# A fused sigmoid attention and top-1 expert layer: when first weights are loaded, which queue loads keys and values, where the item list is built, and when gate sums are issued

## The chip, the cores and the metric

The kernel runs on one core of a Trainium2 chip. The metric is the device time of one execution in microseconds (us), as a median of several runs. The core has a matrix engine (TensorE, "PE" in the profile; its weight loads are "PEld"), a vector engine (VectorE, "DVE"), an activation engine (ScalarE, "ACT"), a general engine (GpSimd, "POOL") and a sync engine (SyncE, "SP") that here only issues DMAs. Every engine executes its own instructions strictly in the order in which the program gave them to it, and waits where an instruction's inputs or its output buffer are not ready. "SPq" and "POOLq" (or POOL with DMA_DIRECT2D) in the profile are DMA issues by SP and by GpSimd.

## What is computed

```python
scores = q @ k.T / sqrt(64) - log(448)          # 8 batches, 12 heads, 448 x 64
x = sigmoid(scores) @ v                         # -> 3584 tokens of 768
logits = x @ w_gate                             # 8 experts
e = argmax(logits);  g = softmax(logits)[e]
out = g * (relu(x @ w1[e]) @ w2[e])             # 768 -> 1024 -> 768
```

## The kernel before

**Attention** (`attention`, L605) works on 48 pairs of heads, two pairs at a time: 24 units `u` of 7 steps each (`ST` = 7), 168 steps `s`. A step computes one seventh of the keys for two pairs: 8 score matmuls (L561), two sigmoids on ACT (L546), 8 value matmuls (L577). Pair `g` needs its keys and queries loaded (L509, four DMAs of 56 KB for each of the two), transposed by DVE (`turn`, L530), and its values loaded (L522, two DMAs of 112 KB). `READY` (L598) issues these by place in the unit: at `i` = 0 and 3 it turns keys of the next unit and loads keys and queries of the unit after that; at `i` = 1 and 4 it turns queries and loads values of the next unit. Keys, queries and values have four buffers each. `K_POOL` (L591) is the pair below which keys and values are issued by GpSimd instead of SP; queries are always SP's. In the steps before `START` = 70 only attention is computed, two steps at a time (even `s`); from then on it is interleaved with the experts' products.

**Gate.** When a unit ends, ACT and DVE split its output (L585, L586: `sh`, `sl`), DVE transposes it into token rows (L462) that SP stores (L466), and `gate_a` (L261) adds its part of the logits: four matmuls (L266) into a PSUM tile and one DVE instruction (L271 or L273) into `g16`. `stages_late` calls it at `i` == 2 of the next unit for `s` >= 70, `stages_early` by another rule before. After three units a batch `b` is done, and the stages b, c, c2, l, c3, d, d2, g, e (`stage`, L637) choose its commonest expert, rank the tokens, scatter records of them to DRAM (L392, four indirect DMAs of GpSimd), and read the batch's whole slot of tokens back (`load_slot`, L429: SP reads two register values, then issues four DMAs of 336 KB into `raw`). The PSUM tiles of the scores and of the gate stages come from one ring of four.

**Slots.** Seven slots follow, each one batch's worth of tokens with one expert's weights (`moe`, L200). A slot has 288 products (matmuls of 128x128 by 448): 8 groups of 18 for the first layer (L216), then three times two groups of 24 for the second (L239). After a first-layer group ACT and DVE make `hh` and `hl` (L223, L224); after a second-layer group DVE scales and transposes it (L251, L252). Groups alternate between two PSUM tiles, so the engine work after a group may take as long as the next group's matmuls before PE waits. `split_tokens` (L441) makes the token parts of the next slot: a DVE transpose into `whole` (two buffers), a cast, a subtraction; the first slot's subtractions are GpSimd's (L452), at the steps of `SPLITS` (L594).

**Weights** (`Weights`, L138) go through five buffers `wst`: `load(n)` issues SP DMAs (L159, 384 KB; L128, 512 KB) until n pieces are loaded, `ahead(n)` splits pieces until n are split (ACT cast L135, GpSimd subtraction L136) and keeps five loads in front of the piece being split. A load into a buffer waits until the subtraction that reads it is done. The first call, `ahead(0)`, comes with stage l of batch 1 (step 52), right behind that slot's four token DMAs; `FIRST` (L593) then splits three pieces at steps 63, 66 and 69.

**Order.** The generator `mo` runs all 7 x 288 = 2016 products, and the program takes from it by hand: `more(n)` issues the next n products, `until(n)` issues products until n are left. Each step from 70 on takes 14 (`MIX`), in two halves of seven, which leaves 490 when attention ends. `gate_a` and the other stages of a step with `i` > 0 are issued between the two halves.

**Item list.** Tokens whose expert is not their slot's are handled at the end as items of 256 rows. DVE builds the list of items on 128x112 tables: two running scans (L788), comparisons, sums (L790 to L805); PE moves it to one row (L809), DVE writes it as integers `li` (L811) and clears the row buffers (L991, L992). All engines read the count from it, SP the item numbers; SP loads two items' records (L847), GpSimd gathers token rows with two indirect DMAs for each (L827), DVE sorts them (`sort_large`, copies L851), and `split_rows` transposes and splits them (L866 to L871). This is issued with 470 (scans), 450, 430, 422 and 412 products left; the first item's gathers with 400 and 388 left; its sort with 330 left, the second item's gathers with 318 and 306, the splits with 288, 270 and 252, the second sort with 234. Two items, computed by `large`, and a loop for any others end the kernel.

Of the kernel before, what the change touches and what calls it, by code (L numbers as in the profile page):

```python
# [24 lines left out]
def tile_sigmoid_attention_top1_moe(  # L25
# [112 lines left out]
    class Weights:  # L138


        LOADS, PARTS = KF + NU // 2, KF + NU
# [354 lines left out]
    def load_pair(g):  # L496
        if g >= NG:
            return
        b, hp = divmod(g, NP)
        for nm, src in (("k", k), ("q", q)):  # L500
            t = apool.tile([P, S // 32, 32], F32, tag=nm + "n", bufs=4, name=f"{nm}n_{g}")
            for h in range(2):
                for f in range(D // 32):
                    a = 2 * h + f
                    if nm == "q":
                        eng = nc.scalar if g == 0 or g == 1 and a < 2 else nc.sync
                    else:
                        eng = nc.gpsimd if 1 <= g < K_POOL else nc.sync
                    eng.dma_start(  # L509
                        t[32 * a : 32 * (a + 1)],  # L510
                        src[b, 2 * hp + h, :, 32 * f : 32 * (f + 1)].rearrange("(j r) s -> r j s", r=32),
                    )
            ops[g, nm + "n"] = t

    def load_values(g):
        if g >= NG or (g, "v") in ops:
            return
        b, hp = divmod(g, NP)
        t = apool.tile([P, KC, D], F32, tag="vn", bufs=4, name=f"vn_{g}")
        for h in range(2):  # L520
            eng = nc.gpsimd if 4 <= g < K_POOL else nc.sync
            eng.dma_start(t[quarter(g, h)], v[b, 2 * hp + h].rearrange("(p c) d -> p c d", c=KC))  # L522
        ops[g, "v"] = t

    def turn(g, nm):

        if g >= NG:
            return
        t = apool.tile([P, S], F32, tag=nm + "t", bufs=4, name=f"{nm}t_{g}")
        nc.vector.transpose(t, ops.pop((g, nm + "n")).rearrange("p j s -> p (j s)"))  # L530
        ops[g, nm] = t

    def warm_up(n):

        ps = ps_moe.tile([P, 512], F32, tag="moe", name="ps_warm")
        for _ in range(n):
            nc.tensor.matmul(ps[:, :P], ones, ones, start=True, stop=True)
# [3 lines left out]
    ST = KC  # L541
    N_ST = NG // 2 * ST
# [9 lines left out]
    def scores(s):  # L552
        u, c = divmod(s, ST)
        two = [2 * u + n for n in range(2)]
        pss = [score_tile(f"{g}_{c}") for g in two]
        for g, ps in zip(two, pss):
            if s == 0 and g == 1:
                warm_up(FILL)
            for h in range(2):
                ks = ops[g, "k"][OWN[h]].rearrange("d (p c) -> d c p", c=KC)[:, c]  # L560
                nc.tensor.matmul(ps[quarter(g, h), :S], ks, ops[g, "q"][OWN[h]], start=True, stop=True)  # L561
        for g, ps in zip(two, pss):
            squash(g, c, ps)
# [24 lines left out]
            for g, pv in pvs:  # L588
                tokens(g, pv)

    WARM, FILL, K_POOL = 60, 20, 18  # L591
    START = 70
    FIRST = {START - 7: 1, START - 4: 2, START - 1: 3}  # L593
    SPLITS = (START - 10, START - 9, START - 7, START - 6, START - 4, START - 3)  # L594
    PB = NP // 2 * ST
    MIX = (7, 7)
# [8 lines left out]
    def attention():  # L605

        order = ExitStack()
        order.enter_context(tc.manual_schedule())
        warm_up(WARM)
        load_pair(0)  # L610
        load_pair(1)
        for g in range(2):
            turn(g, "k")
            turn(g, "q")
            load_values(g)
        nc.gpsimd.dma_start(wg, w_gate.rearrange("(t p) e -> p t e", p=P))
        setup()
        for g in (2, 3):
            load_pair(g)
            load_values(g)  # L620
        done_av = done_sc = 0

        def weigh_to(n):
            nonlocal done_av
            while done_av < min(n, N_ST):
                weighted(done_av)
                done_av += 1

        def score_to(n):
            nonlocal done_sc  # L630
            while done_sc < min(n, N_ST):
                scores(done_sc)
                done_sc += 1

        gate = {}

        def stage(what, b):  # L637
            g = gate.setdefault(b, {})
            if what == "b":
                g["oh"], g["z"] = gate_b(b)  # L640
            elif what == "c":
                g["c"] = gate_c(b, g["oh"], g["z"])
            elif what == "c2":
                g["lm"] = gate_c2(b, g["oh"], *g["c"])
            elif what == "c3":
                gate_c3(b, *g["c"][:2])
            elif what == "l" and b > 0:
                load_slot(b - 1, g["c"][2])
                if b == 1:
                    wts.ahead(0)  # L650
            elif what == "d":
                g["si"] = gate_d(b, g["lm"])
            elif what == "d2":
                gate_d2(b, g["si"])
            elif what == "g" and b > 0:
                g["gs"] = gate_g(b - 1)
            elif what == "e" and b > 0:
                gate_e(b - 1, g["gs"])

        LATE = {3: "b", 7: "c", 8: ("l", "c2"), 9: "c3", 10: "d", 12: ("d2", "g"), 14: "e"}  # L660
        LAST = {3: "b", 5: "c", 6: ("l", "c2"), 7: "c3", 8: "d", 9: ("d2", "g"), 10: "e"}
        EARLY = {5: "b", 7: ("c", "c2"), 9: ("l", "c3"), 11: "d", 13: ("d2", "g"), 15: "e"}
        FIRST_LATE = {5: "b", 10: "c", 11: ("l", "c2"), 12: "c3", 14: "d", 16: ("d2", "g"), 17: "e"}
        PLACES = {}
        for b in range(B):
            for r, what in (EARLY, EARLY, FIRST_LATE, LATE, LATE, LATE, LATE, LAST)[b].items():
                at = (b + 1) * PB + r
                at += at < START and at % 2
                PLACES.setdefault(at, []).extend((w, b) for w in ((what,) if isinstance(what, str) else what))

        summed = {}

        def stages_early(s):
            for u in range(START // ST):
                if summed.get(u) == s - 2:
                    gate_a(u)
            for w in PLACES.get(s, ()):
                stage(*w)

        def stages_late(s):  # L680
            u, i = divmod(s, ST)
            if i == 2 and u - 1 not in summed and u <= N_ST // ST:
                gate_a(u - 1)
            for w in PLACES.get(s, ()):
                stage(*w)

        for s in range(N_ST + 11):
            u, i = divmod(s, ST)
            a = u * ST
            if s in FIRST:  # L690
                wts.ahead(FIRST[s])
            if s < START:
                if s % 2 == 0:
                    weigh_to(min(s - 1, (done_av // ST + 1) * ST))
                    if done_av and done_av % ST == 0:
                        summed.setdefault(done_av // ST - 1, s)
                    stages_early(s)
                    score_to(s + 2)
            elif i == 0:
                stages_late(s)  # L700
                score_to(a + 2)
                weigh_to(a)
                score_to(a + 4)
            yield s, MIX[0]
            if s >= START:
                if i > 0:
                    stages_late(s)
                if i == 3:
                    weigh_to(a + 2)
                    score_to(a + 6)  # L710
                    weigh_to(a + 4)
                    score_to(a + 7)
                    weigh_to(a + 5)
            if s == 8:
                nc.gpsimd.tensor_copy(wgs[:, :, 0:E], wg)
                nc.gpsimd.tensor_sub(wgs[:, :, E : 2 * E], wg, wgs[:, :, 0:E].bitcast(F32))
            if i in READY and s < N_ST:
                READY[i](u)
            if s in SPLITS:
                split_tokens(0, SPLITS.index(s))  # L720
            yield s, MIX[1]
        order.close()

    wts = Weights([(lambda b=b: regs.get(b)) for b in range(B + 1)])
# [8 lines left out]
    def more(n):  # L733
        nonlocal left
        for _ in range(min(n, left)):
            next(mo)
            left -= 1

    def until(n):
        more(left - n)  # L740
# [42 lines left out]
    nc.vector.tensor_scalar(cut(0), cut(0), float(TS), None, op0=ALU.add)  # L783
    nc.vector.tensor_tensor(ek(4), ek(0), n_rec, op=ALU.is_lt)
    nc.vector.tensor_sub(few, few, big)
    more(20)
    for msk, cum in zip((big, few), rank):
        nc.vector.tensor_tensor_scan(cum, cut(3), msk, 0.0, op0=ALU.mult, op1=ALU.add)  # L788
    ends = rest.tile([P, 1], F32, name="ends")
# [211 lines left out]
    for get in gets[0]:  # L1001
        more(12)
        get()
    until(330)
    by_raw = xpool.tile([P, S // 32, KD, 32], F32R, tag="raw", bufs=1, name="by_raw")
    by_raw = by_raw.rearrange("p j t s -> p (j t s)")
    first = [by_raw[:, n * TL : (n + 1) * TL] for n in range(2 * KD - 2)]
# [84 lines left out]
```

## Time and profile before

| | |
|---|---|
| time, median of 3 runs | 835.1 us (834.96 to 835.94) |
| the profiled execution | 836.3 us; from its first to its last instruction 834.5 us |
| mean granted PE clock | 0.987 |
| busy: PE, PEld, DVE, ACT, POOL | 96%, 73%, 48%, 47%, 42% |
| DMA | 124.07 MB, mean 149 GB/s |
| first product of the slots (L216) starts | 153.10 us |
| last product of the slots (L239) starts | 755.99 us |

PE is busy nearly throughout, so time is won or lost where PE stands still. The table by stretches, the list of waits of PE and the timeline of single engines show those places; an engine's own wait is shown in brackets behind its instruction, with what ended it. Rows of the timeline that hold several instructions of a kind ("x4") give the whole run's length.

### The profile page before, as it was taken

To read this page: it belongs to the slowest core of one execution; us is meant where nothing else is said; L and a number is where in the kernel's file an instruction comes from. 1 tells how busy PE (TensorE), PEld (TensorE's weight loads), DVE (VectorE), ACT (ScalarE), POOL (GpSimd) and SP (SyncE) were. 2 spreads that over 40 slices of the span, in tenths; PEclk is the share of its full clock that TensorE was granted. 3 is DMA by queue.
4 is the path that set the end of the run, shared out by engine and by line. 5 is a ranking of instruction groups with operands and counts; after the bars stand their busy time and mean duration, and the time that the engine had idled before them with its cause. 6 is when DMAs were issued, how large, how long until landed. Compare 5 with 4: busy or idle time off the path is not lost. (4 is left out here: it accounts for less than half of the span.)

```text
span 834.5 us, 15673 instructions
## 1 busy us (share of the span) xinstructions
PE 805.0 (96%) x5568; PEld 612.9 (73%) x5568; DVE 400.0 (48%) x861; ACT 388.2 (47%) x709; POOL 349.6 (42%) x328
## 2 busy tenths in 40 slices
PE   9999986999999999999999999999999799999996
PEld 6545442777867876777768768777788698999996
DVE  2454644362546327453354525574276765224533
ACT  5676653563545536444544445356333233334441
POOL 9756324234332632235223333334354445565250
PEclk9999998999999999999999999999999899999998
DMA  9685698577477756488473983855267446546670
GB/s 193 141 182 120 153 180 180 125 155 183 104 172 148 187 117 148 108 186 169 116 167 78 194 199 93 183 129 152 72 154 171 127 113 165 157 107 167 199 217 35
DMA packets 324595, 124.07 MB, mean 149 GB/s; under 512 B 222174, under 2 KB 322478, under 8 KB 324512
## 3 DMA queue, kind: packets, MB, share of 16 engines
q1 hardware_dynamic: 316448, 112.52, 59.2%
q0 software_dynamic: 5280, 10.15, 4.2%
q8 instruction: 45, 0.74, 0.4%
q10 hardware_dynamic: 2784, 0.34, 0.3%
q14 instruction: 38, 0.31, 0.1%
HBM read 100.89 MB, written 22.48 MB: 148 GB/s over the span
## 5 line engine op out<-in xcount | busy, mean ns | idle before, releaser
L546 ACT ACTIVATE at<-sc,bias_s 128x448 f32<-128x448 f32 x336 | 188.1, 641 | 152.3 <-PE sc L561 151.4
L136 POOL TENSOR_TENSOR w1l<-wst,w1h 128x768 fp32r<-128x768 f32 x72 | 132.2, 1844 | 209.4 <-ACT w1h L135 195.0
L136 POOL TENSOR_TENSOR w2l<-wst,w2h 128x512 fp32r<-128x512 f32 x84 | 106.7, 1290 | 174.2 <-ACT w2h L135 169.4
L577 PE MATMUL av<-at,vn 64*64 64x448 f32 x1344 | 164.5, 545 | 6.9 <-DMA vn<-in_v_dram 6.9
L561 PE MATMUL sc<-qt,kt 64*64 64x448 f32 x1344 | 167.5, 553 | 3.7 <-DVE g L273 2.9
L216 PE MATMUL ps<-xh,w1h 128*128 128x448 f32 x336 | 124.7, 371 | 6.8 <-DVE hl L224 6.3
L561 PEld LDWEIGHTS sc<-qt,kt 64*64 64x64 f32 x1344 | 82.1, 193 | 60.8 <-issue 32.7
L239 PE MATMUL ps<-hh,w2h 128*128 128x448 f32 x336 | 123.3, 367 | 1.0 <-DVE ob L252 1.0
L216 PE MATMUL ps<-xl,w1h 128*128 128x448 f32 x336 | 124.0, 369 | 0.0
L216 PE MATMUL ps<-xh,w1l 128*128 128x448 f32 x336 | 123.9, 369 | 0.0
L239 PE MATMUL ps<-hh,w2l 128*128 128x448 f32 x336 | 123.5, 367 | 0.3 <-POOL w2l L136 0.3
L239 PE MATMUL ps<-hl,w2h 128*128 128x448 f32 x336 | 123.1, 366 | 0.0
L577 PEld LDWEIGHTS av<-at,vn 64*64 64x64 f32 x1344 | 60.6, 134 | 68.5 <-issue 45.9
L135 ACT CAST w2h<-wst 128x512 fp32r<-128x512 f32 x108 | 65.2, 622 | 58.4 <-PE ps L239 45.0
L223 ACT ACTIVATE hh<-ps 128x448 fp32r<-128x448 f32 x56 | 30.6, 547 | 122.8 <-PE ps L216 122.8
L251 DVE TENSOR_TENSOR ps<-ps,gt 128x448 f32<-128x448 f32 x42 | 26.4, 629 | 122.7 <-PE ps L239 122.6
L224 DVE SCALAR_TENSOR_TENSOR hl<-ps,hh 128x448 fp32r<-128x448 f32 x56 | 34.7, 619 | 93.2 <-ACT hh L223 93.2
L216 PEld LDWEIGHTS ps<-xh,w1h 128*128 128x128 f32 x336 | 63.5, 189 | 15.8 <-DVE hl L224 7.1
L239 PEld LDWEIGHTS ps<-hh,w2h 128*128 128x128 f32 x336 | 65.2, 194 | 8.8 <-issue 4.1
L239 PEld LDWEIGHTS ps<-hh,w2l 128*128 128x128 f32 x336 | 65.2, 194 | 7.0 <-issue 3.0
L239 PEld LDWEIGHTS ps<-hl,w2h 128*128 128x128 f32 x336 | 65.2, 194 | 6.6 <-issue 3.3
L216 PEld LDWEIGHTS ps<-xl,w1h 128*128 128x128 f32 x336 | 63.5, 189 | 8.8 <-issue 3.5
(163 smaller groups left out, 1008.4 us busy)
## 6 DMA issues: line engine op xcount, KB each, us to landing
wst<-in_moe_w_dram SPq DMA_DIRECT2D x72, 384.0 KB, 3.5
wst<-in_moe_w_dram SPq DMA_DIRECT2D x54, 512.0 KB, 4.4
x_tok<-xt SPq DMA_DIRECT2D x64, 168.0 KB, 2.9
qn<-in_q_dram SPq DMA_DIRECT2D x186, 56.0 KB, 2.6
raw<-x_tok SPq DMA_DIRECT2D x28, 336.0 KB, 6.5
out_dram<-ob SPq DMA_DIRECT2D x84, 112.0 KB, 2.4
vn<-in_v_dram SPq DMA_DIRECT2D x68, 112.0 KB, 3.5
kn<-in_k_dram SPq DMA_DIRECT2D x124, 56.0 KB, 3.0
```

The lines of the kernel that those rows point to most:

```text
L135: nc.scalar.copy(hi, st)
L136: eng.tensor_tensor(lo, st, hi.bitcast(F32), op=ALU.subtract)
L216: nc.tensor.matmul(ps[:, :S], a[:, ws], b_, start=(t == 0 and n == 0), stop=(t == KD - 1 and n == 2))
L223: nc.scalar.activation(hh[:, :S], ps[:, :S], AF.Relu)
L224: nc.vector.scalar_tensor_tensor(hl[:, :S], ps[:, :S], 0.0, hh[:, :S].bitcast(F32), op0=ALU.max, op1=ALU.subtract)
L239: nc.tensor.matmul(ps[:, :S], a, b_, start=(j == 0 and n == 0), stop=(j == KF - 1 and n == 2))
L251: nc.vector.tensor_tensor(ps[:, :S], ps[:, :S], gate_rows[b], op=ALU.mult)
L546: nc.scalar.activation(at, ps[:, :S], AF.Sigmoid, bias=bias_s, scale=SCALE)
L561: nc.tensor.matmul(ps[quarter(g, h), :S], ks, ops[g, "q"][OWN[h]], start=True, stop=True)
L577: nc.tensor.matmul(psv[g][OWN[h], :S], ops[g, "v"][rows, c, :], at[rows], start=(c == 0), stop=(c == KC - 1))
```

## The change

Four things differ. First, the first weights: stage l of batch 1 no longer calls `ahead(0)`. Instead five single loads are issued at steps 55, 58, 61, 63 and 65 (`LOADS`), and the three first splits come at steps 65, 67 and 69. Second, GpSimd issues the keys and values of pairs up to 21 instead of 17 (`K_POOL` 22). Third, the scans of the item list are issued with 330 products left instead of 470, and all that follows keeps its distances (310, 290, 282, 272; gathers with 260 and 248 left) up to the first sort, in front of which `until(330)` becomes `more(14)`: the sort comes with 234 left, the second item's gathers with 222 and 210, the splits with 192, 174 and 156, the second sort with 138. Fourth, `stages_late` calls `gate_a` at `i` == 1, one step (14 products) sooner.

```diff
-    WARM, FILL, K_POOL = 60, 20, 18
+    WARM, FILL, K_POOL = 60, 20, 22
     START = 70
-    FIRST = {START - 7: 1, START - 4: 2, START - 1: 3}
+    LOADS = (START - 15, START - 12, START - 9, START - 7, START - 5)
+    FIRST = (START - 5, START - 3, START - 1)
...
                 load_slot(b - 1, g["c"][2])
-                if b == 1:
-                    wts.ahead(0)
...
         def stages_late(s):
             u, i = divmod(s, ST)
-            if i == 2 and u - 1 not in summed and u <= N_ST // ST:
+            if i == 1 and u - 1 not in summed and u <= N_ST // ST:
                 gate_a(u - 1)
...
+            if s in LOADS:
+                wts.load(LOADS.index(s) + 1)
             if s in FIRST:
-                wts.ahead(FIRST[s])
+                wts.ahead(FIRST.index(s) + 1)
...
     nc.vector.tensor_sub(few, few, big)
-    more(20)
+    until(330)
     for msk, cum in zip((big, few), rank):
         nc.vector.tensor_tensor_scan(cum, cut(3), msk, 0.0, op0=ALU.mult, op1=ALU.add)
...
         more(12)
         get()
-    until(330)
+    more(14)
```

## The prediction, made before the changed kernel ran

> **What bounds the kernel now.** The page's row of PE by slices first, then windows where it drops, then PE's waits.
>
> ```profile
> PE   9999986999999999999999999999999799999996
> ```
> ```profile
> 99.60:115.30 15.70, 15.70 (x140) 1.00 0.96 189
> 115.30:153.05 37.75, 27.52 (x214) 0.91 0.77 160
> ```
> ```profile
> PE av L577 <- DMA vn<-in_v_dram: 6.9, 1, 6.9
> PE ps L216 <- DVE hl L224: 6.3, 2, 5.9
> PE sc L561 <- DVE g L273: 2.9, 1, 2.9
> PE pl L278 <- DVE g L273: 2.0, 2, 1.6
> ```
>
> PE is nearly always busy, so only its pauses are to be had. Four matter: two in the second window (6.9 and 2.9), where PE is busy for 27.52 of 37.75 us and the granted clock falls to 0.91; one of 5.9 in the tail; one of 1.6 at a gate sum. (A window's row has length, PE's busy time and instructions, granted clock, DMA share, GB/s; a wait's row total, times, longest.) The change touches all four.
>
> The first two, followed back through SP's timeline and DVE's:
>
> ```profile
> 101.18 1.92 SPq L435 DMA_DIRECT2D raw<-x_tok  x4
> 103.29 9.76 SPq L159 DMA_DIRECT2D wst<-in_moe_w_dram  x5
> 113.35 3.76 SPq L509 DMA_DIRECT2D kn<-in_k_dram  x4
> ...
> 133.69 1.11 SPq L522 DMA_DIRECT2D vn<-in_v_dram  x2
> 135.07 0.41 SPq L159 DMA_DIRECT2D wst<-in_moe_w_dram  x1
> ```
> ```profile
> 119.79 0.65 DVE L530 STREAM_TRANSPOSE kt<-kn 128x448 f32<-128x448 f32 x1 [6.27 <-DMA kn<-in_k_dram]
> ```
>
> Five weight loads hold SP for 9.76 us, where one alone takes 0.41. Behind them pair 19's keys are issued at 113.35; DVE waits for them 6.27 us, the gate sum stands behind that transpose, and PE waits 2.9. From there SP issues nearly without a pause and does not catch up: pair 19's values go out at 133.69, and PE waits 6.9 for them. So it is the order and pace of SP's queue that ends last here.
>
> **The change, part by part.** *First weights and pairs 18 to 21.* What it can be worth comes from the two windows: the one just before the stall, and the one up to the slots' first product. In the first, 140 matmuls of attention and gate took 15.70 us, 0.112 each. The 214 of the second would take 24.0 us at that pace, not 37.75: **13.7 us**, and the first product would start at 139.4 instead of 153.1. That is more than the two waits (9.8), since the slow clock goes too.
>
> Does nothing else come late? GpSimd's costs by line (20 to 100 us), its timeline, and the page's landing time:
>
> ```profile
> L509 POOL DMA_DIRECT2D kn<-in_k_dram x46 | 29.4, 656 | 1.8 <-DMA kn<-in_k_dram 0.9 <-DVE sl L586 0.9
> L522 POOL DMA_DIRECT2D vn<-in_v_dram x28 | 15.1, 551 | 22.0 <-PE av L577 13.5 <-PE pc L315 7.0 <-DMA kn<-in_k_dram 1.1
> ```
> ```profile
> 95.63 2.08 POOL L522 DMA_DIRECT2D vn<-in_v_dram  x4 [7.03 <-PE pc L315]
> ...
> 111.12 0.97 POOL L392 DMA_INDIRECT recs<-rec,si  x1 [0.30 <-issue]
> 123.72 1.14 POOL L452 TENSOR_TENSOR xl<-whole,xh 128x448 fp32r<-128x448 f32 x1 [11.64 <-DVE xh L451]
> ...
> 126.85 1.82 POOL L136 TENSOR_TENSOR w1l<-wst,w1h 128x768 fp32r<-128x768 f32 x1 [0.52 <-ACT w1h L135]
> ```
> ```profile
> vn<-in_v_dram POOLq DMA_DIRECT2D x28, 112.0 KB, 4.0
> ```
>
> Added to GpSimd are 16 key DMAs (16 x 0.656 = 10.5 us) and 8 value DMAs (8 x 0.551 = 4.4). Pairs 18's and 19's keys fall in the time around 95.63 in which GpSimd only waits, and are there before 105. Pairs 20's and 21's come behind the four scatters (the last ends at 112.1), which themselves wait for the ranks. Then two groups of keys and pairs 18's and 19's values take 2 x 2.6 + 2 x 1.1 = 7.4: issued by 119.5, landed 4.0 later at 123.5. PE wants them at step 66; step 60 begins at 115.3, and three double steps of 32 matmuls (3.6 each) later it is 126.1. It fits by 2.6. Next come two more values (2.2), six token subtractions (6 x 1.14 = 6.8) and three weight subtractions (3 x 1.82 = 5.5): 134.0, before 139.4. Queued behind a value load that waits for its buffer are those subtractions; for them wait the first products, and SP, whose sixth weight load needs the first subtraction's buffer. Behind that wait on SP stand keys and queries of pair 23, not turned before step 73. I count none of these, and 13.7 stays. Its ends: 7.5, if the transfers keep the pace they had (a rival, below), and 13.7, since nothing else may be late. Without its cover a late value costs PE what it is late.
>
> *Gate sums a step sooner.* PE's and DVE's timeline:
>
> ```profile
> 423.21 0.36 PE L266 MATMUL psg<-sh,wgs 128*16 128x448 f32 x1
> 423.41 0.37 PE L266 MATMUL psg<-sl,wgs 128*16 128x448 f32 x1
> ...
> 428.04 0.56 DVE L273 TENSOR_TENSOR g<-g,psg 16x448 f32<-16x448 f32 x1
> ...
> 428.65 0.42 PE L278 MATMUL pl<-ident,g 16*128 16x16 f32 x4 [1.61 <-DVE g L273]
> ...
> 429.00 2.56 PE L577 MATMUL av<-at,vn 64*64 64x448 f32 x16
> ...
> 431.32 2.62 PE L561 MATMUL sc<-qt,kt 64*64 64x448 f32 x16
> ...
> 433.75 1.68 PE L577 MATMUL av<-at,vn 64*64 64x448 f32 x16
> ```
>
> The sum stood in DVE's queue until 428.04, though its matmuls began at 423.21. 14 products (0.20 us each, by the starts of the two L266 rows) sooner is 2.8 us: more than the 1.61 of the wait, so it goes, and with it the slow groups behind it (2.56 and 2.62 against 1.68): 1.61 + 0.88 + 0.94 = **3.4**. The rest of L278's waits (0.4) I count at nothing: what DVE does next is late there anyway. The new wait would be PE's for `sl`, which now has 21 products (4.3 us) of cover instead of 35; for its two casts and two subtractions that is enough, so nothing. Ends 0 and 3.4.
>
> *The scans later.* The scans' own row, GpSimd beside them, the end of the list's sums; then ACT, GpSimd, DVE and PE where the scans are put:
>
> ```profile
> L788 DVE TENSOR_TENSOR_SCAN w2s<-w2s x2: 360/5282/10203, 647.0 to 657.1; 128x112 f32<-128x112 f32 x2
> ```
> ```profile
> 650.74 6.18 POOL L136 TENSOR_TENSOR w2l<-wst,w2h 128x512 fp32r<-128x512 f32 x5
> ```
> ```profile
> 660.13 0.15 DVE L803 TENSOR_SCALAR lf<-lf 128x1 f32<-128x1 f32 x1
> ```
> ```profile
> 689.30 2.29 ACT L135 CAST w1h<-wst 128x768 fp32r<-128x768 f32 x3
> ...
> 690.21 1.84 POOL L136 TENSOR_TENSOR w1l<-wst,w1h 128x768 fp32r<-128x768 f32 x1 [0.73 <-ACT w1h L135]
> ...
> 690.63 0.65 DVE L252 STREAM_TRANSPOSE ob<-ps 128x448 f32<-128x448 f32 x1
> ...
> 695.73 0.36 PE L239 MATMUL ps<-hh,w2h 128*128 128x448 f32 x1
> ```
>
> The second scan took 0.36 us; the first 10.2, ending as GpSimd's unbroken row of subtractions did (650.74 + 6.18 = 656.92). So it was blocked, not slow. At the new place (330 left) DVE reaches the scans at 691.2, on the clock of before, behind that L252, while three weight subtractions, all cast by 691.6, fill GpSimd from 690.21 to 695.8. I take it that the scan waits for their end again. The list's sums end 2.8 us after the scans (657.5 to 660.3); 0.6 more for L251 and L252 in place of one `hl`, 0.6 for the scans: 699.8. PE needs them with 290 products left, where 695.73 stands: idle 4.1. Before it was 5.9; the slow matmuls after either I take as equal: **1.8** gained. Ends: 5.9 (a gap is found) and -3.5 (a block as long as before). The Trainium skill, SBUF — State Buffer, section Who interferes with whom, says that a VectorE instruction with two SBUF inputs and a GpSimd one that reads SBUF exclude each other, for one whole instruction. By that alone a scan would enter between two subtractions, and the idle would be about 1 us less; the first scan's 10.2 us over several of them disagree.
>
> Without the gathers (L827) among the last slot's token splits, DVE is less late there; I add **1.0** for short waits before the new place (ends 0 and 1.3).
>
> *The first sort.* It now follows the second gather by 14 products (2.8 us) instead of 58. Gathers and sort copies, then ACT and GpSimd in that slot:
>
> ```profile
> L851 DVE COPY w2s<-xg x4: 547/904/2212, 691.2 to 707.9; 128x768 f32<-128x768 f32 x4
> ...
> DMA to landing us min/median/max: 4.3/4.4/4.5
> ```
> ```profile
> 712.52 0.54 ACT L223 ACTIVATE hh<-ps 128x448 fp32r<-128x448 f32 x1 [2.38 <-PE ps L216]
> ```
> ```profile
> 713.86 1.84 POOL L136 TENSOR_TENSOR w1l<-wst,w1h 128x768 fp32r<-128x768 f32 x1 [1.80 <-ACT w1h L135]
> ```
>
> The second gather queues on GpSimd behind a weight subtraction that ends 3.2 us after its group's `hh` began (712.52 to 715.70). It lands 4.4 later, the copy takes 0.55, and behind it on DVE stands the next group's `hl` (0.6), for whose PSUM tile PE waits: with 0.3 of hand-overs 9.1 us after that `hh`. PE wants it two groups on, 36 x 0.20 less the 0.2 by which `hh` trails: 7.1. A new idle of 2.0, with 0.6 for a slower clock behind it: **-2.6**. Ends 0 and -5.9 (both copies at their longest, 2.2). Moved along at no cost: the clears of the row buffers, two record loads on SP, the second item's splits and sort, which keep at least 48 products to their inputs.
>
> **Sum**: 13.7 + 3.4 + 1.8 + 1.0 - 2.6 = 17.3. The profiled execution took 836.3 (834.5 of span, 1.8 around it), 1.2 above the median of 835.1: 819.0 in its own terms, **817.8** as a median.
>
> **Rivals.**
> - *Transfers set the pace at START* (0.15). For it: the DMA share of 0.96 in the first window; against it: 0.77 in the second, while PE stood still. Up to the first product some 7.6 MB must move (token read, six weight loads, the pairs' loads, two token stores, by their sizes). At the windows' mean of about 172 GB/s that takes 44 us from 101.2: 145.6, so 7.5 gained instead of 13.7: **824**. The Trainium skill, DMA: Bandwidth & Descriptors, section Issuing engines are not separate DMA queues, takes this side: several issuers only save issue time, usually small. SP's 9.76 us for five issues is not small.
> - *The tail is free* (0.15): the scans find GpSimd idle and the gather is in time; 4.1 + 2.6 more: **811**.
> - *The tail is worse* (0.12): scans blocked as long as before; 5.3 less: **823**.
> - *GpSimd's queue holds the first product: slower* (0.04). Each value load may wait for its buffer; the waits seen sum to 22.0, one of them 7.0. Four of 7.0 put 28 us before the subtractions: 134.0 becomes 162, the first product 9 later than before, and with the rest **841**. It decides from some 23 us of added waits.
> - *The loads are spread but SP stays full* (0.04), the token read alone holding it, and queries come late as keys did: 2.9 lost again, **821**.
>
> The forecast itself has 0.50, and 814 to 822 as its own range; with the rivals and the unknown ends it is **811 to 826**. 0.2% is about what a measurement of this kernel can tell from no change: faster 0.94, same 0.02, slower 0.04.
>
> **What would show it.** Right: no wait of PE for `vn` or `g` at 100 to 140, the first L216 near 139, L509 and L522 of GpSimd there; no wait of L278 at 410; a PE wait of some 4 us with 290 products left; one of 2 for `hl` four groups into the last slot. Wrong: a first product after 145, a new PE wait for `kt` or `w1l`, or tail waits above 8 us together.

## The result, and the profile after

The changed kernel takes 815.74 us (median of four runs, 814.98 to 818.63) against 835.52 of the kernel before on the same chip: a ratio of 0.9767 (0.9739 to 0.9795). The forecast was 817.8. The profiled execution took 814.98, with a span of 813.2. It is the fastest of the four, 0.8 under their median; that of before (836.3) lies 0.8 above this 835.52, and 1.2 above the 835.1 that the prediction went by. So the two traces differ by 1.5 more than the medians do.

First the page of the changed kernel: PE by slices, and the clock granted to it.

```profile
PE   9999999999999999999999999999999988999996
...
PEclk9999999999999999999999999999999999999999
```

The gaps of before (86 in slices 6 and 7, the 7 in slice 32) are gone, and a shallow new one stands in slices 33 and 34. Next the windows of PE at the start of the slots (length, busy and instructions, clock, DMA share, GB/s):

```profile
99.60:115.30 15.70, 15.70 (x140) 1.00 0.91 179
115.30:139.00 23.70, 23.24 (x213) 1.00 1.02 226
```

The same 213 or 214 matmuls that took 37.75 us take 23.70, at a granted clock of 1.00, and the transfers now run at 226 GB/s instead of 160. Then PE's waits (total, times, longest):

```profile
PE pli L810 <- issue: 3.0, 1, 3.0
PE ps L216 <- DVE hl L224: 2.5, 2, 2.2
PE ps_warm L537 <- POOL ones L75: 1.0, 1, 1.0
PE sc L561 <- DVE lg L292: 0.9, 2, 0.6
PE ps L216 <- DVE xt L462: 0.5, 1, 0.5
```

The waits for `vn` (6.9), for `g` (2.9 and 2.0) and the 5.9 for `hl` are gone. Two are new: 2.95 for the list's matmuls, and 2.2 for `hl` behind the first sort.

To see where the time went I compare the start of the same product (L216 and L239 in PE's timeline, counted from the first) in the two traces. The number is by how much it starts sooner in the changed kernel:

| product | sooner by, us | what lies since the row above |
|---|---|---|
| 1 | 14.1 | first weights, pairs 18 to 21 |
| 800 | 14.4 | |
| 900 | 17.8 | the gate sum at 428 |
| 1566 | 18.1 | |
| 1604 | 26.3 | the scans' old stall is gone |
| 1710 | 28.2 | short waits of the last layer are gone |
| 1800 | 24.0 | the list's new wait |
| 1878 | 20.1 | the sort's new wait |
| 2016 | 20.1 | |

Between them these rows also hold work that only moved: three groups of transposes (`px`, 0.36 us each, 1.1 together) ran between products 1710 and 1800 before, and run between 1800 and 1878 now. Set right for them, the list cost 28.2 - 24.0 + 1.1 = 5.3, the sort 24.0 - 20.1 - 1.1 = 2.8. The list's own four matmuls (L810, 0.6) moved too, from between products 1566 and 1604 to between 1710 and 1800: 0.6 of the 8.2 gained there, and 0.6 of the 5.3 lost, are theirs.

After the slots PE's work takes the same time in both. The spans differ by 1.2 more than these 20.1: from the last scatter's issue to the end it was 834.5 - 827.54 = 7.0 before, and is 813.2 - 807.46 = 5.7 now. That is not chance: it is 6.95 in all five traces with `K_POOL` 18, and 5.7 to 6.0 in all eight with 22, the one in which nothing else was changed among them (5.9). The scatter lands 3.3 us after its issue began in both; what is shorter is a `DRAIN` of GpSimd at the kernel's end, the longest of these three (shortest, median and longest in ns), before and after:

```profile
L1087 POOLq DRAIN  x3: 46/115/6356, 827.3 to 834.2; - x3
```
```profile
L1088 POOLq DRAIN  x3: 46/115/5096, 807.2 to 812.9; - x3
```

So a microsecond at the end comes with the keys and values on GpSimd, and the prediction had no term for it. Why, no run shows.

### The profile page after: what moved, and what is told of

It is laid out like the page before. It is cut to its first block, busy times and chain, and to the rows that moved or that the text cites. A ratio compares the mean times of both kernels' runs of the same rounds, so it can differ in the third digit from the quotient of the medians.

```text
span 813.2 us, 15675 instructions
## 1 busy us (share of the span) xinstructions
PE 798.7 (98%) x5568; PEld 612.5 (75%) x5568; DVE 395.5 (49%) x861; ACT 388.1 (48%) x709; POOL 364.7 (45%) x352
## 5 line engine op out<-in xcount | busy, mean ns | idle before, releaser
L561 PE MATMUL sc<-qt,kt 64*64 64x448 f32 x1344 | 163.7, 550 | 1.0 <-DVE lg L292 0.9
L577 PE MATMUL av<-at,vn 64*64 64x448 f32 x1344 | 158.7, 539 | 0.0
L216 PE MATMUL ps<-xh,w1h 128*128 128x448 f32 x336 | 124.6, 371 | 2.9 <-DVE hl L224 2.5
L216 PE MATMUL ps<-xl,w1h 128*128 128x448 f32 x336 | 124.2, 369 | 0.0
L216 PE MATMUL ps<-xh,w1l 128*128 128x448 f32 x336 | 124.1, 369 | 0.0
L239 PE MATMUL ps<-hh,w2h 128*128 128x448 f32 x336 | 123.2, 367 | 0.0
L239 PE MATMUL ps<-hl,w2h 128*128 128x448 f32 x336 | 123.2, 367 | 0.0
L239 PE MATMUL ps<-hh,w2l 128*128 128x448 f32 x336 | 123.1, 366 | 0.0
L216 PEld LDWEIGHTS ps<-xh,w1h 128*128 128x128 f32 x336 | 63.6, 189 | 12.4 <-DVE hl L224 3.2
L239 PEld LDWEIGHTS ps<-hl,w2h 128*128 128x128 f32 x336 | 65.2, 194 | 7.1 <-issue 3.5
L239 PEld LDWEIGHTS ps<-hh,w2h 128*128 128x128 f32 x336 | 65.2, 194 | 7.1 <-issue 3.5
L216 PEld LDWEIGHTS ps<-xh,w1l 128*128 128x128 f32 x336 | 63.6, 189 | 8.9 <-issue 2.6
L216 PEld LDWEIGHTS ps<-xl,w1h 128*128 128x128 f32 x336 | 63.5, 189 | 8.6 <-issue 3.5
```

Of the source, the lines that this page charges most:

```text
L216: nc.tensor.matmul(ps[:, :S], a[:, ws], b_, start=(t == 0 and n == 0), stop=(t == KD - 1 and n == 2))
L239: nc.tensor.matmul(ps[:, :S], a, b_, start=(j == 0 and n == 0), stop=(j == KF - 1 and n == 2))
L577: nc.tensor.matmul(psv[g][OWN[h], :S], ops[g, "v"][rows, c, :], at[rows], start=(c == 0), stop=(c == KC - 1))
```

## The experiments

Gains by product are meant as in the table above, against the trace of before. The kernel before was timed beside each group: 834.89 with the first four, 839.01 with the shift and the three after the rows, 835.78 with the rows and the last two. Chips differ by that much, so a time is read by its ratio.

### The loads alone

```diff
-    FIRST = {START - 7: 1, START - 4: 2, START - 1: 3}
+    LOADS = (START - 15, START - 12, START - 9, START - 7, START - 5)
+    FIRST = (START - 5, START - 3, START - 1)
...
-                if b == 1:
-                    wts.ahead(0)
...
+            if s in LOADS:
+                wts.load(LOADS.index(s) + 1)
             if s in FIRST:
-                wts.ahead(FIRST[s])
+                wts.ahead(FIRST.index(s) + 1)
```

> The kernel before with only the weight loads spread; pairs 18 to 21 stay on SP. Theory (SP's pace): the five loads held SP 9.76 us in a row and five single ones take 5 x 0.41 = 2.1, so SP gets 7.7 back, the rest of its queue is as full as before: first product near 145.4 instead of 153.1, about 828 us. Rival (the burst alone makes the stall): first product near 139, about 821 us. Rival (SP stays full, values late again): first product above 150, about 833 us.

828.8 us, ratio 0.992 (0.9903 to 0.9938); first product at 147.06, 6.0 sooner. Windows and waits of this kernel:

```profile
115.30:147.06 31.76, 25.78 (x213) 0.89 0.79 179
```
```profile
PE av L577 <- DMA vn<-in_v_dram: 5.5, 1, 5.5
```

The keys come in time, so the wait for `g` is gone, but SP's queue is as full as before behind it, and the values are late again. The theory held, 1.7 short of its 7.7.

### Pairs 18 to 21 alone

```diff
-    WARM, FILL, K_POOL = 60, 20, 18
+    WARM, FILL, K_POOL = 60, 20, 22
```

> The kernel before with only pairs 18 to 21's keys and values on GpSimd; the five weight loads stay one behind the other. Theory (SP's pace): SP loses 4 x (3.76 + 1.11) = 19.5 us of issues, so the wait for values (6.9) goes with the slow clock; queries of pair 19 now stand behind the five loads where keys stood, so some of the 2.9 stays: first product at 141 to 144, about 824 to 826 us. Rival (the burst decides): a wait of 2.9 or more for queries and the loads late behind it, first product above 148, about 831 us. Rival (no burst needed, issuers decide): first product near 139, about 821 us.

823.29 us, ratio 0.9856 (0.9839 to 0.9872); first product at 142.09, 11.0 sooner. SP's timeline, then DVE's, of this kernel:

```profile
102.76 9.31 SPq L159 DMA_DIRECT2D wst<-in_moe_w_dram  x5
112.17 7.32 SPq L509 DMA_DIRECT2D qn<-in_q_dram  x8
```
```profile
121.49 0.65 DVE L530 STREAM_TRANSPOSE qt<-qn 128x448 f32<-128x448 f32 x1 [4.98 <-DMA qn<-in_q_dram]
```

As expected the queries stand where the keys stood: DVE waits 4.98 for them and PE 1.7 behind it. The five loads still cost, but less. The median gained 11.6, a little more than the 9 to 11 expected; about 1 of its trace's gain lies at the end, as said above. The two parts overlap: 6.0 and 11.0 alone, 14.1 together.

### The gate sums alone

```diff
-            if i == 2 and u - 1 not in summed and u <= N_ST // ST:
+            if i == 1 and u - 1 not in summed and u <= N_ST // ST:
```

> The kernel before with only the gate sums a step sooner. Theory: the wait of 1.6 for g at 428 and the slow groups behind it go, 3.4 us: about 831.7 us, and product by product no difference elsewhere. Rival (the wait moves to the casts sl, or to the next thing DVE is late with): 0 to 1.6 us, 833.5 to 835.

Two readings that do not agree. In its trace the gain from product 800 to 900 is 3.44, as forecast, and no wait of PE over 0.3 is new in it. But the median is 833.68 against 834.89, a ratio of 0.9982 (0.9970 to 0.9995): 1.2 us, at most 2.5, which is in the rival's range. The next experiment gives part of the reason: it keeps the old gate sums, and has the same wait at the same place. First before, then the kernel with the scans alone, windows of PE. They are cut where the granted clock can change in that trace, which is every 3.41 us (the last section shows from what):

```profile
426.36:429.77 3.41, 1.80 (x16) 1.00 0.87 221
429.77:433.19 3.42, 3.42 (x24) 0.50 0.97 254
```
```profile
424.39:427.80 3.41, 2.37 (x12) 1.00 0.85 187
427.80:431.21 3.41, 2.84 (x32) 1.00 0.89 229
```

In both PE stands still for 1.61 us. Before, all of it lies in one stretch of 3.41 us, in which PE is busy for 1.80, and the next stretch runs at half the clock: half of 3.41 is lost, 1.7. In the other trace the wait lies across the end of a stretch, PE is busy for 2.37 and 2.84, and the clock stays at 1.00. In the other three traces that keep this wait (the two experiments above, the shift below) it lies whole in a stretch too, with PE busy for 0.53 of it, and one stretch at 0.50 follows. So 1.6 of the 3.4 is there each time, and the other 1.7 or 1.8 only where the wait falls so. That is not the whole reason: if it falls so in four executions of five, some 3.0 is to be expected (an estimate from these traces), more than the 2.5. The traces compared are also the fastest of this kernel's ten executions (832.12) and a slow one of before; the rest is open.

### The scans alone

```diff
     nc.vector.tensor_sub(few, few, big)
-    more(20)
+    until(330)
...
         get()
-    until(330)
+    more(14)
```

> The kernel before with only the scans 160 products later and the first sort 14 products behind the second gather. Theory (three signed terms: the old stall of 5.9 with its slow matmuls is worth 7.4, short waits 1.9, the new list wait with its slow matmuls costs 4.2, the new sort wait 2.6): 2.5 us gained, about 832.6 us. Rival (the tail's moves are worth what was forecast, 1.8 + 1.0 - 2.6): 0.2 us, about 835 us. Rival (the tail's gain comes only with the earlier start, which changes how GpSimd and DVE meet): no gain or a loss.

834.74 us, ratio 0.9997 (0.9984 to 1.001): no difference. That fits the rival with the forecast's own 0.2, and as well the one by which the gain comes only with the earlier start. By product 8.2 come from the old stall (1.8 to 10.0) and 1.9 from the short waits; then both new waits take 9.5 (11.9 to 2.4), against 8.1 in the changed kernel's trace. The waits themselves are the same to 0.2 (2.95 and 2.38, there 2.95 and 2.22); what differs is the clock behind the second, one stretch of 3.41 us at 0.50 here and none there. The later place takes away a stall and makes two that cost as much.

### What blocks a scan

The first scan of before took 10.2 us and ended with GpSimd's row of subtractions; in the changed kernel the two scans took 1.1 and 2.0 beside such a row. One difference was seen between the two traces: before, the scan began at 646.97, inside GpSimd's last scatter issue (646.14 to 647.12). The first test moves its start behind that issue:

```diff
     more(20)
+    nc.vector.memset(xgs, 0.0)
     for msk, cum in zip((big, few), rank):
...
     nc.vector.memset(xg, 0.0)
-    nc.vector.memset(xgs, 0.0)
```

> The kernel before with one 0.70 us clear (xgs) moved ahead of the first scan, so that the scan begins some 0.7 us later, inside GpSimd's first weight subtraction instead of inside the DMA issue before it. Theory (a VectorE instruction that begins while GpSimd issues a DMA gets no turn until the row of subtractions ends; one that begins inside a subtraction enters at the next boundary): both scans end by about 651 instead of 657, PE's wait for hl of 5 to 5.9 falls under 1, about 829 to 830 us. Rival (the length of the row decides): the scans end at the row's end as before, the wait grows by 0.5, no change or slower. Rival (chance from run to run): the wait falls in this look, the times spread as before.

838.35 against 839.01, ratio 1.000 (0.9981 to 1.0018); PE's wait is 5.06, so it neither fell under 1 nor grew. GpSimd's and DVE's timeline, and the scans by their shortest, mean and longest in ns:

```profile
648.82 3.66 POOL L136 TENSOR_TENSOR w1l<-wst,w1h 128x768 fp32r<-128x768 f32 x2
652.42 6.38 POOL L136 TENSOR_TENSOR w2l<-wst,w2h 128x512 fp32r<-128x512 f32 x5
```
```profile
649.48 8.25 DVE L789 TENSOR_TENSOR_SCAN w2s<-w2s 128x112 f32<-128x112 f32 x2
```
```profile
L789 DVE TENSOR_TENSOR_SCAN w2s<-w2s x2: 1379/4166/6952, 649.5 to 656.4; 128x112 f32<-128x112 f32 x2
```

The scan began inside the first subtraction and still waited 7.0, past four boundaries between subtractions. The theory that a start inside a DMA issue is needed falls. Nor did the shift change anything in a whole kernel: the kernels with the loads, the pairs and the gate sums alone keep the scans where they were. There the first scan begins inside the scatter's issue as before, and yet it gets its turn behind the fifth of the row's seven subtractions, the very place at which the shifted one does. In the kernel with the pairs alone:

```profile
L788 DVE TENSOR_TENSOR_SCAN w2s<-w2s x2: 1383/4549/7715, 635.8 to 643.4; 128x112 f32<-128x112 f32 x2
```

PE's wait is 5.0 to 5.1 in these three. So the 10.2 and the 5.9 that the prediction started from are what this one execution of before showed. The second test measures the row by itself, on tiles of its own ahead of the changed kernel's work. Four forms run three times each; "early" and "late" are as "ready", with six casts on ACT in front of the row or one in front of each subtraction:

```diff
...
+        def start():
+            nc.gpsimd.tensor_copy(go, cum[1])
+        def scans():
+            for c in cum:
+                nc.vector.tensor_tensor_scan(c, one, go, 0.0, op0=ALU.mult, op1=ALU.add)
+        def low(n, h):
+            nc.gpsimd.tensor_tensor(lows[n], src, highs[h].bitcast(F32), op=ALU.subtract)
+        def ready():
+            start()
+            scans()
+            for n in range(6):
+                low(n, n)
...
+        def issue():
+            start()
+            scans()
+            nc.gpsimd.dma_start(aside, one)
+            for n in range(6):
+                low(n, n)
```

> The changed kernel with four probes ahead of its first work, three times each: two scans (128x112) on VectorE that begin as a row of six GpSimd subtractions (128x512) begins. Forms: inputs ready long before (ready); the six casts that feed the row done before it (early); each cast ending while the subtraction before its own runs (late); a DMA issue between the scans' start and the row (issue). Theory A (a waiting VectorE instruction enters at a boundary only where GpSimd's next instruction was not yet ready when the one before it began): in late the first scan waits for one subtraction, in ready, early and issue for the whole row. Theory B (it enters at the next boundary whatever is ready): one subtraction in all four forms. Theory C (a start inside a DMA issue decides): the whole row in issue alone. Theory D (any of these, by chance): the three repeats of a form differ.

The timeline of DVE and GpSimd in the third repeat of "ready", and in the second of "issue" (L84 are the subtractions, L108 the DMA issue, L81 the two scans):

```profile
20.39 7.53 POOL L84 TENSOR_TENSOR lo<-src,hi 128x512 fp32r<-128x512 f32 x6
...
20.46 2.74 DVE L81 TENSOR_TENSOR_SCAN cum<-one,go 128x112 f32<-128x112 f32 x2 [4.97 <-POOL go L77]
```
```profile
86.84 0.56 POOL L108 DMA_DIRECT2D aside<-one  x1 [0.20 <-issue]
87.42 7.35 POOL L84 TENSOR_TENSOR lo<-src,hi 128x512 fp32r<-128x512 f32 x6
...
86.68 8.35 DVE L81 TENSOR_TENSOR_SCAN cum<-one,go 128x112 f32<-128x112 f32 x2 [0.44 <-POOL go L77]
```

In eight of nine repeats without the issue, each scan enters at the next boundary, whether the casts were early or late: the two together take 2.74 or 2.75 (2.19 in one that began 0.6 into the first subtraction). In all three with the issue a scan waits out the whole row: 8.42, 8.35 and 8.31. In the second and third of these the first scan, begun before the issue, took 0.39, and the second, begun inside it, 8.0. Theory A falls (late makes no difference), B falls (issue does), C holds for these eleven. The twelfth, the first repeat of "ready", began 3.4 us into its row and waited 4.2 to the row's end without any issue beside it, unlike the other two of its form, which is what theory D looks for. So in the probes a scan that began inside GpSimd's DMA issue lost every turn of the row behind it, three times of three. In whole kernels it did so in the trace of before, but not in the three with 7.7 to 7.8 us, which lost four turns inside the row as the shifted scan did. No run separates one more rival: that it matters whether the row follows directly behind a DMA issue, and not where the scan begins. The row did so in all of these, the shift among them, and in none of the eight repeats that got their turns; the first repeat of "ready" speaks against it. What decides stays open.

### The two new waits apart

Each from the changed kernel; the sort further from its gather, the list's matmuls later, and both with the scans sooner:

```diff
         get()
-    more(14)
+    more(40)
```

> The changed kernel with the first sort 40 instead of 14 products behind the second gather. Theory (the sort copies stand ahead of hl on DVE while the gather lands): PE's wait of 2.2 with 200 to 210 products left goes, with 1.5 of slow matmuls behind it where the clock fell: 2.2 to 3.7 gained, 812 to 813.5 us. Rival (the wait moves to the next item's gathers or to the last slot's end, for px or xl): under 1 us gained.

```diff
-    more(20)
+    more(34)
     pli = ps_x.tile([P, 512], F32, tag="px", name="pli")
```

> The changed kernel with the list's matmuls (pli) 14 products later, so 2.8 us. Theory (PE waits there for lf alone, 2.95): 2.8 to 3.8 gained, the wait at pli under 0.3, about 812 to 813 us. Rival (SP's reads of the list come late, and with them the record loads, gathers and the sort): the sort's wait grows by what pli gains, no change.

```diff
-    until(330)
+    until(350)
...
-    more(20)
+    more(34)
     pli = ps_x.tile([P, 512], F32, tag="px", name="pli")
...
         get()
-    more(14)
+    more(40)
```

> The changed kernel with both, and the scans 20 products sooner (350 left instead of 330), so that they meet GpSimd between two single w2 subtractions and not in its row of three. Theory: neither wait is left, no PE idle over 0.5 from 640 to the end of the slots, 5 to 7 gained: 809 to 811 us. Rival (the scans meet another row): a new wait of PE for hl or ob of 2 or more, 812 to 814 us.

815.14, 816.97 and 814.88 us against 839.01 of the kernel before: ratios of 0.9713 (0.9690 to 0.9736), 0.9731 (0.9709 to 0.9754) and 0.9704 (0.9682 to 0.9726), all three overlapping the changed kernel's own interval or close under it. By ratio the first lies some 4 us under the changed kernel (0.9767 above, 0.9758 below), as its theory has it, but the two were not timed side by side. Between products 1744 and 2016 the sort's stall is gone in the first: the gain only changes from 21.8 to 21.3, where the changed kernel lost 3.3. In the second the list's wait goes, but 1.3 comes back as a wait for the PSUM tile that DVE frees behind the list's sums, and the sort's is still 1.8: a miss. In the third both are gone, and the earlier scans meet the token splits instead: three waits of 0.7 (for `w2h`, `w2l` and `ob`), and 22.9 falls to 19.8 between products 1680 and 1728. That is its rival, under another name.

### The list later still

The last two ran side by side, the changed kernel and its sort and list both later:

> The changed kernel itself, beside the next one on the same chip: 0.974 to 0.980 of the kernel before, with the list's wait of about 3 and the sort's of about 2.2.

```diff
-    until(330)
+    until(290)
...
         get()
-    more(14)
+    more(40)
```

> The changed kernel with the scans 40 products later still (290 left), where GpSimd stands idle for 11 us, and the sort 40 products behind the gather. Theory (both new waits come from places, not from work: the list and the sort are free where their inputs meet an idle GpSimd and a landed gather): no PE wait for pli, no wait of 2 for hl, 4.5 to 7 less than the changed kernel, 0.969 of the kernel before or below. Rival (the list's results then come late for SP's reads, the record loads and the gathers): a new wait at the sort or at the item's first matmuls, less than 3 gained.

The changed kernel: 815.91, ratio 0.9758 (0.9741 to 0.9776). This one: **808.05**, ratio 0.9668 (0.9652 to 0.9684), 7.9 us under the changed kernel, and the best of all. PE's waits:

```profile
PE ps_warm L537 <- POOL ones L75: 1.0, 1, 1.0
PE sc L561 <- DVE lg L292: 0.9, 2, 0.6
PE sc L561 <- DVE qt L530: 0.8, 2, 0.7
PE ps L216 <- DVE xt L462: 0.4, 1, 0.4
PE ps L216 <- DVE hl L224: 0.2, 1, 0.2
```

No wait is left that the tail makes. But not for the reason in the expectation. The timeline of GpSimd, DVE and PE:

```profile
662.38 5.52 POOL L136 TENSOR_TENSOR w1l<-wst,w1h 128x768 fp32r<-128x768 f32 x3 [0.74 <-ACT w1h L135]
```
```profile
664.74 3.41 DVE L789 TENSOR_TENSOR_SCAN w2s<-w2s 128x112 f32<-128x112 f32 x2
...
671.48 0.15 DVE L804 TENSOR_SCALAR lf<-lf 128x1 f32<-128x1 f32 x1
```
```profile
676.44 0.60 PE L810 MATMUL pli<-ident,lf 128*1 128x128 f32 x4
```

The scans met the same row of three subtractions as in the changed kernel, and took 3.4 instead of 3.0. What changed is that the sums are ready at 671.6 and PE asks for them at 676.4, 4.8 later. The sort's distance was changed with it, so the 7.9 is not the list's alone.

## Why the prediction was right

**What bounds.** SP's order and pace set the first product, as said: taking 24 issues off SP alone brought 11.0, spreading the loads alone 6.0. 13.7 was forecast from the pace of matmuls without a stall, 14.1 came, and the first product started at 138.99 instead of 139.4. The rival that the transfers set the pace is out: at 226 GB/s they kept up, with a DMA share of 1.02, and PE was busy for 23.24 of the 23.70 us. The Trainium skill, DMA: Bandwidth & Descriptors, section Issuing engines are not separate DMA queues, calls the issue time that several issuers save usually small; here moving issues alone was worth 11.0 us, so the trace differs. GpSimd's chain had less room than forecast; its timeline in the changed kernel:

```profile
118.03 1.09 POOL L522 DMA_DIRECT2D vn<-in_v_dram  x2
...
126.56 1.13 POOL L452 TENSOR_TENSOR xl<-whole,xh 128x448 fp32r<-128x448 f32 x1 [2.28 <-DMA kn<-in_k_dram]
...
135.01 1.82 POOL L136 TENSOR_TENSOR w1l<-wst,w1h 128x768 fp32r<-128x768 f32 x1
```

The loads end at 119.1 (forecast 119.5), the last subtraction at 136.8 (forecast 134.0), 2.2 before the first product. The lateness is not a value load waiting for its buffer, which the prediction named and counted at nothing. The subtractions waited four times, 3.3 together, for DVE's casts, and the forecast's sum set them one behind the other. That holds for the wait of 2.28 too: the cast that it needs ends on DVE at 126.47, and no wait for a key load stands in front of that.

**The gate sums.** 3.4 in the trace, as forecast, and no new wait for `sl`. As a term for the median it was too large: 1.2 when made alone. One step that failed is to count the slow groups behind a wait as if they came with it each time; it does not account for all of the difference.

**The scans later**: forecast 1.8, measured 8.2 - 5.3 = 2.9. Two steps of it were off. The row of three subtractions was met as forecast, but the scans did not wait for its end. The changed kernel's timeline and the scans' lengths:

```profile
662.04 5.61 POOL L136 TENSOR_TENSOR w1l<-wst,w1h 128x768 fp32r<-128x768 f32 x3 [0.73 <-ACT w1h L135]
```
```profile
663.03 2.99 DVE L789 TENSOR_TENSOR_SCAN w2s<-w2s 128x112 f32<-128x112 f32 x2
...
670.62 0.15 DVE L804 TENSOR_SCALAR lf<-lf 128x1 f32<-128x1 f32 x1
```
```profile
L789 DVE TENSOR_TENSOR_SCAN w2s<-w2s x2: 1100/1532/1965, 663.0 to 664.1; 128x112 f32<-128x112 f32 x2
```

The first ends at 664.13, just behind the first subtraction (662.04 + 1.85), the second just behind the second, and PE waits 2.95 instead of 4.1. The Trainium skill, SBUF — State Buffer, section Who interferes with whom, gives this: by its one whole instruction the idle was to be 1 us less, and 4.1 - 2.95 = 1.15. It does not give the 10.2 of before. The second step is that I took the slow matmuls behind both as equal: 8.2 - 5.9 = 2.3 went, 5.3 - 2.95 = 2.3 came, and 0.6 of each is the list's own matmuls, so 1.7 and 1.7. In this execution that was right; it too hangs on the clock. And the 5.9 is one execution's: three other traces with the old place have 5.0 to 5.1, with which the same sum would have come to 0.9 or 1.0.

**Short waits**: forecast 1.0, with 1.3 as an end; 1.9 measured. The three waits that went make 0.3 + 0.3 + 0.7 = 1.3; the other 0.6 I cannot place by a wait.

**The first sort**: forecast 2.0 idle and 2.6 in all; measured 2.2 and 2.8. The changed kernel's timeline shows the chain as it was worked out:

```profile
684.40 1.05 POOL L828 DMA_INDIRECT xg<-x_tok,rec  x1 [0.15 <-issue]
```
```profile
689.54 0.56 DVE L852 COPY w2s<-xg 128x768 f32<-128x768 f32 x1 [3.18 <-DMA xg<-x_tok,rec]
690.01 1.15 DVE L224 SCALAR_TENSOR_TENSOR hl<-ps,hh 128x448 fp32r<-128x448 f32 x2
```

The gather lands, the copy follows, and two groups' `hl` stand behind it; PE goes on at 690.7. The idle time was forecast by its mechanism, the 0.6 behind it only by its size: it was to come from a slower clock, and here the clock stayed at 1.00. In the changed kernel's second trace (the list later still) a stretch at 0.50 does follow, and the sort costs 4.3.

**The sum.** 17.3 forecast, 20.1 found in the slots, and 1.2 at the end that had no term. Of the 2.8 between them 0.4 is the first product, 1.1 the scans and 0.9 the short waits, the sort takes 0.2 off, and the other 0.6 are small differences over the slots that no row names. These are two single executions; in the changed kernel's second trace the slots gain 18.5. In medians 815.74 came against 817.8, inside 814 to 822, a gain of 19.8. The parts do not add up to it: 14.1 for the first product, 1.2 at the end, 1.2 for the gate sums and 0.2 for the tail, the last two as medians of the parts made alone, make 16.7. The other 3 show only with all of them together, and no run says where; the intervals of the ratios leave each of these medians a microsecond or two. So the first product was forecast by its mechanism; that the small terms came to the right total is in part luck.

## What to carry to other kernels

A queue that issues without a pause delays whatever is asked of it last, so look for the issues in front of a late transfer, and move or spread those, not the late one alone. A chain of small steps for a later stage cost nothing here where its consumer asked late; give the consumer distance first (4.8 us here was worth 7.9 with the sort's), and only then look for an undisturbed place for the steps. When you price a stall, keep the wait and the slow matmuls behind it as two terms, and treat the second (1.7 here) as one that may or may not come. And read a wait in more than one trace before you build on its length.

## What the runs showed of the hardware

**The clock behind a short wait depends on where the wait falls.** In the record of all 13 traces the granted clock is either 1.00 or 0.50, and between two changes lies a whole number of stretches of 3.41 us (in the trace of before 37, 2, 85, 1, 65, 2 and 49). Where these stretches begin, counted from the kernel's first instruction, differs from trace to trace. Cut so, the traces hold 3011 stretches at 1.00 after their first 20 us. In 28 of them PE was busy for less than 0.45 of the time, and a stretch at 0.50 followed each time; in 2971 it was busy for more than 0.60, and none followed; of the 12 between, it followed 6. So the same 1.6 us of standing still brought half the clock in four traces, where it lay whole in one stretch, and none in the fifth, where it lay across two. The sort's wait, first in the changed kernel's first trace, then in its second:

```profile
685.83:689.24 3.41, 2.63 (x13) 1.00 0.98 268
689.24:692.65 3.41, 1.97 (x10) 1.00 0.90 296
```
```profile
687.91:691.32 3.41, 1.26 (x7) 1.00 0.86 246
691.32:694.73 3.41, 3.41 (x11) 0.50 0.99 296
```

This is read from traces; no run moved a wait against the stretches on purpose. The Trainium skill, TensorE: Matmul & The Clock Gate, section HAM oscillation — how this bites in real kernels, names idle gaps above about 3.4 us as those to avoid; here half of that was enough. The clock also fits the spread of the times: beside the last group the kernel before ran from 834.17 to 838.18, and the one without waits in its tail from 807.89 to 808.34. That the clock makes this spread was not tested by itself.

**A VectorE scan (two SBUF inputs) can miss turn after turn of a GpSimd row**: 8.0 to 8.1 us behind six subtractions when it began inside a DMA issue in front of them, four turns of a row of seven in four whole kernels, one subtraction at a time in eight of nine repeats without an issue. What decides stays open.
